# Retention attention regrouped into units of one batch and four heads, issued in a written-out software pipeline with the routing in pieces between

## The chip, the cores and the metric

The kernel runs on one core of a Trainium2 chip. The metric is the device time of one execution in microseconds (us), lower is better. The core has a matrix engine (PE, with its weight loads shown apart as PEld), a vector engine (DVE), an activation engine (ACT), a general engine (POOL) and a queue engine (SP). Each takes its instructions in the order in which they were issued to it. Matmuls write to PSUM, which has eight banks of 128 partitions by 2 KB; DVE and ACT read it, POOL does not in this kernel.

## The reference

The first half is a causal retention over 8 batches, 8 heads, 576 positions and a head dimension of 64. The second half sends each of the 4608 resulting rows of 512 to two of eight small networks.

```python
scores = scale * np.matmul(q, k.transpose(0, 1, 3, 2))
Dmat = np.where(rel >= 0, gamma[:, None, None] ** rel[None, :, :], 0.0)
attn = np.matmul(scores * Dmat, v)              # 8, 8, 576, 64
x = attn.transpose(0, 2, 1, 3).reshape(4608, 512)
logits = x @ w_gate
noisy = logits + np.log1p(np.exp(x @ w_noise)) * noise
top2 = np.argpartition(-noisy, 2, axis=1)[:, :2]
...
    h = np.maximum(x[mask] @ w1[e], 0.0)        # 512 -> 1024
    out[mask] += top2_w[mask, k, None] * (h @ w2[e])
```

## The kernel before

There are two stages. The first reads q, k and v, computes the retention and the routing, and writes the rows, with their routing data, to a scratch array `xd`. The second (`experts`, L581) goes through 40 tiles of 256 rows, five per network: it gathers the rows of a tile from `xd`, multiplies by both weight matrices, and scatters the result.

**Attention.** The work is cut into 16 units, a pair of batches (`bp`) by a pair of heads (`hp`). The decay is split into a factor on v (table `vg`) and a factor on the output (table `gt`), so scores need only a causal mask. The first 512 positions of a head are four chunks of 128; the last 64, the tail, go with both batches in one block. Position 256c + 2p + r lies in partition p (0 to 127) of the loaded tile, so one loaded partition holds two neighbouring positions, and a chunk of 128 positions lies in 64 partitions. `stage_a` (L164) therefore moves data between partition halves while it casts to bf16: eight POOL instructions per unit make `kn` (L180), two on POOL and two on DVE make `vn` (L184), two on ACT make `qb` (L188). It then transposes q and k on PE and copies them out with ACT (L203, L210). `stage_b` (L218) makes the scores S (L230) and masks them on DVE (L233), and makes the running key-value state T per batch (L247), which ACT copies out block by block (L253). `stage_c` (L257) adds, per chunk, vn times S (L272, two 64-column matmuls) and state times q (L275) in PSUM, and DVE writes it out times `gt` as `xT` (L277). The tail has its own small instructions in every unit (L192 to L194, L212 to L215, L239, L240, L282 to L287).

**Routing.** After every fourth unit `route` (L313) takes one `xT` of 1152 rows: 36 small matmuls (L322), a long chain of small DVE instructions, nine POOL additions that depend on each other (`cum`, L368), wide one-hot compares (L432 to L440), 18 matmuls that sum into one PSUM tile `pT` (L443), and for each of nine blocks four transposes, an ACT copy, a POOL copy and a DMA to `xd` (L449 to L453). After the last one `finish` (L455) and `overflow_list` (L466) make the lists.

**Order.** In the attention and the routing a scheduler orders the instructions of each engine by its own priorities, so the order in the source isn't the order on the chip: the trace shows instructions of `route` among those of later units, and the weight loads of the first three networks (`load_weights`, L788, called at units 7, 9 and 11) are issued from 23.45 us on. All q, k and v loads and the writes to `xd` go through SP's queue. In `experts` the order is written out by hand (`manual_schedule`, L740), except for eleven DVE memsets ahead of it (L598, L600). There the weights of networks 3 to 7 come through a staging buffer (`wload`, L605) and ACT casts (`wcast`, L621); the first five tiles load none.

PSUM tiles by name and number of buffers: `tr` 2 (transposes), `S` 2, `x` 2, `T` 1 (states, and the small results of the routing), `pT` 1.

Of the kernel before, what the change touches and what calls it, by code (L numbers as in the profile page):

```python
# [39 lines left out]
def constants(nc, cp):  # L40
# [47 lines left out]
def decay_tables(nc, cp, tmp):  # L88

    vg = cp.tile([P, 4, 2, 2, 2, 2], F32, name="vg")  # L90
# [8 lines left out]
    nc.gpsimd.iota(sv, pattern=[[1, 2], [256, 2]], base=0, channel_multiplier=2,  # L99
# [16 lines left out]
class Attention:  # L116
    def __init__(self, tc, ctx, K, q, k, v):
# [5 lines left out]
        self.raw = ep("at_raw", 2)  # L123
# [5 lines left out]
        self.vg, self.vgt, self.gt = decay_tables(nc, self.cp, self.bf)  # L129
        self.Tb = [self.cp.tile([P, 4, P], BF16, name=f"Tb{j}") for j in range(4)]  # L130
        for t in self.Tb:
            nc.gpsimd.memset(t, 0.0)
        self.u = {}
        self.tails = {}
        self.mains = {}
        self.xT = {}

    def load(self, u):
        nc = self.nc
        bp, hp = u // 4, u % 4  # L140
        d = {}
        for n in "qkv":
            a = self.src[n]
            if hp % 2 == 0:
                r = self.raw.tile([P, 2, 2, 4, P], F32, name=f"raw_{n}")
                for b in range(2):
                    for c in range(2):
                        nc.sync.dma_start(  # L148
                            out=r[:, b, c],
                            in_=a[2 * bp + b, 2 * hp:2 * hp + 4, 256 * c:256 * c + 256, :].rearrange(  # L150
                                "h (p r) d -> p h (r d)", r=2))
                self.mains[n] = r
            d[n] = self.mains[n][:, :, :, (hp % 2) * 2:(hp % 2) * 2 + 2, :].rearrange("p b c h x -> p (b c) h x")
            if hp == 0:
                t = self.raw.tile([P, 8, HD], F32, name=f"rawt_{n}", bufs=1)
                for b in range(2):
                    nc.sync.dma_start(
                        out=t[b * HD:(b + 1) * HD],
                        in_=a[2 * bp + b, :, 512:, :].rearrange("h s d -> s h d"))
                self.tails[n] = t  # L160
            d[n + "t"] = self.tails[n][:, 2 * hp:2 * hp + 2, :]
        self.u[u] = d

    def stage_a(self, u):  # L164

        nc, K = self.nc, self.K
        V = nc.vector
        d = self.u[u]
        hp = u % 4

        kn = self.bf.tile([P, 2, 4, 2, HD], BF16, name="kn")
        vn = self.bf.tile([P, 2, 4, 2, HD], BF16, name="vn")
        rk = d["k"].rearrange("p c h (r d) -> p c h r d", r=2)
        rv = d["v"].rearrange("p c h (r d) -> p c h r d", r=2)
        for cpar in range(2):
            si = slice(cpar * HD, (cpar + 1) * HD)
            for r in range(2):
                so = slice(r * HD, (r + 1) * HD)
                for h in range(2):
                    nc.gpsimd.affine_select(kn[so, cpar, :, h, :], rk[si, :, h, r, :], pattern=[[0, 4], [0, HD]],  # L180
                                            base=1, channel_multiplier=0, compare_op=Alu.is_gt, fill=0.0)
                g = self.vg[si, hp, r].rearrange("p b c h -> p (b c) h").unsqueeze(3).to_broadcast([HD, 4, 2, HD])
                eng = nc.gpsimd if r else V
                eng.tensor_tensor(vn[so, cpar], rv[si, :, :, r, :], g, Alu.mult)  # L184
        qb = self.bf.tile([P, 4, 2, 2, HD], BF16, name="qb")
        rq = d["q"].rearrange("p c h (r d) -> p c h r d", r=2)
        for r in range(2):
            nc.scalar.activation(qb[:, :, r], rq[:, :, :, r, :], Act.Copy, scale=0.125)  # L188
        qt = self.bf.tile([P, P], BF16, name="qt")
        kt = self.bf.tile([P, P], BF16, name="kt")  # L190
        vt = self.bf.tile([P, 2, HD], BF16, name="vt")
        V.tensor_scalar_mul(qt, d["qt"].rearrange("p h d -> p (h d)"), 0.125)  # L192
        V.tensor_copy(kt, d["kt"].rearrange("p h d -> p (h d)"))
        V.tensor_tensor(vt, d["vt"], self.vgt[:, 2 * hp:2 * hp + 2].unsqueeze(2).to_broadcast([P, 2, HD]), Alu.mult)  # L194

        pq = self.ps.tile([P, 2, 2, 2, 2, HD], BF16, name="tr", bufs=2)
        for b in range(2):
            for cc in range(2):
                for r in range(2):
                    nc.tensor.transpose(pq[:, b, cc, :, r, :],  # L200
                                        qb[:, 2 * b + cc, r].rearrange("p h d -> p (h d)"), K["ident"])
        QT = self.tp.tile([P, 8, P], BF16, name="QT")
        nc.scalar.activation(QT, pq.rearrange("p b c e r q -> p (b c e) (r q)"), Act.Copy)  # L203
        pk = self.ps.tile([P, 8, P], BF16, name="tr", bufs=2)
        knv = kn.rearrange("p e (b c) h d -> p e b c (h d)", b=2)
        for b in range(2):
            for c in range(4):
                nc.tensor.transpose(pk[:, 4 * b + c, :], knv[:, c % 2, b, c // 2, :], K["ident"])
        KT = self.tp.tile([P, 8, P], BF16, name="KT")
        nc.scalar.activation(KT, pk, Act.Copy)  # L210
        pt = self.ps.tile([P, 2, P], BF16, name="tr", bufs=2)
        nc.tensor.transpose(pt[:, 0, :], qt, K["ident"])  # L212
        nc.tensor.transpose(pt[:, 1, :], kt, K["ident"])
        TT = self.tp.tile([P, 2, P], BF16, name="TT")
        V.tensor_copy(TT, pt)  # L215
        d.update(kn=knv, vn=vn.rearrange("p e (b c) h d -> p e b c h d", b=2), vt=vt, QT=QT, KT=KT, TT=TT)

    def stage_b(self, u):  # L218

        nc, K = self.nc, self.K  # L220
        V = nc.vector
        d = self.u[u]
        ST = {}
        mk = K["mask"].rearrange("p r q -> p (r q)").unsqueeze(1).to_broadcast([P, 4, P])
# [356 lines left out]
def experts(tc, K, wp, w1, w2, keep, xd, yd, out, W):  # L581
# [7 lines left out]
    with tc.tile_pool(name="moe_g", bufs=1) as gp, \  # L589
# [293 lines left out]
```

## Time and profile before

| | us |
|---|---|
| median of 3 runs (lowest, highest) | 652.82 (652.56, 658.53) |
| profiled execution | 652.35 |
| its span, first to last instruction | 650.8 |
| first masked score (DVE L233) | 26.86 |
| last output of the attention (DVE L287) | 287.23 |
| first gather (POOL L632) | 321.62 |
| first expert matmul (PE L677) | 328.95 |

| engine | busy us | share of the span |
|---|---|---|
| PE | 496.8 | 76% |
| PEld | 325.6 | 50% |
| POOL | 355.9 | 55% |
| DVE | 311.5 | 48% |
| ACT | 285.6 | 44% |

A share over the span mixes two stages with different limits; read each from its own stretch. The time ahead of the first and behind the last instruction is the difference of the profiled execution to its span, 1.55 us. Matmul ends are modelled, so the distance between starts says how fast PE goes, and the granted clock is given as a share of 2.4 GHz: 0.50 is 1.2 GHz.

### The profile page before, as it was taken

The page shows a single profiled execution, that of the slowest core. Times are in us where ns is not written, and L with a number is a line of the kernel's source. Part 1 is how long each engine was busy: PE and PEld are TensorE (multiplying, and loading weights), DVE is VectorE, ACT ScalarE, POOL GpSimd, SP SyncE. Part 2 cuts the span into 40 slices and gives each one's busy share as a digit, 9 for nine tenths or more (in the row PEclk, how much of TensorE's full clock was granted, in tenths as well). Part 3 has the DMA queues.
Part 4 walks back from the last instruction along what each step waited for, and adds up shares of the span by engine and source line. Part 5 has one row for each costly group of instructions (what it writes and reads, how often), then busy time and mean ns, then how long its engine had stood idle before and what let it go on. Part 6 is the DMA issues. An engine that isn't in the chain of part 4 may idle for free.

```text
span 650.8 us, 10530 instructions
## 1 busy us (share of the span) xinstructions
PE 496.8 (76%) x3729; PEld 325.6 (50%) x3729; DVE 311.5 (48%) x820; ACT 285.6 (44%) x457; POOL 355.9 (55%) x493
## 2 busy tenths in 40 slices
PE   0583954877468755870389999999899998999990
PEld 0342432634254424540267666676576665666760
DVE  0544478366835684658422234444344443444440
ACT  4622342732154323430234476576466755644430
POOL 5916526361534335201473067777777777777772
PEclk9999999965577555855679999999899998999996
DMA  9999980777037002000233476877868798666551
GB/s 176 263 225 228 223 237 25 213 207 199 0 108 191 20 1 76 1 1 0 93 88 115 143 237 200 263 238 253 270 206 282 259 300 279 217 193 210 181 188 68
DMA packets 112153, 108.60 MB, mean 167 GB/s; under 512 B 28707, under 2 KB 85540, under 8 KB 112097
## 3 DMA queue, kind: packets, MB, share of 16 engines
q1 hardware_dynamic: 86384, 72.51, 37.8%
q0 software_dynamic: 20800, 34.97, 20.1%
q10 hardware_dynamic: 4912, 0.41, 0.6%
q8 instruction: 30, 0.49, 0.3%
q14 instruction: 27, 0.21, 0.1%
HBM read 91.21 MB, written 41.83 MB: 204 GB/s over the span
## 4 chain that ended last, share of the span: by engine, by line
PE 54%; DMA 14%; DVE 10%; issue 7%; POOL 6%; ACT 4%; SPq 3%; ACTq 0%; POOLq 0%; DVEq 0%
PE p L677 20%; PE po L696 19%; DMA raw_v<-in_v_dram 4%; SPq L148 3%; DMA prv<-yd,ix 2%; PE pt L661 2%; PE x L272 2%; POOL kn L180 2%; POOL vn L184 2%; PE S L230 2%; DVE vn L184 2%; PE T L247 2%; DVE S L233 2%; DMA xd<-xr 2%; PE pT L443 1%
## 5 line engine op out<-in xcount | busy, mean ns | idle before, releaser
L677 PE MATMUL p<-xgT,w 128*128 128x256 bf16 x1280 | 246.1, 277 | 0.0
L696 PE MATMUL po<-w,hT 128*128 128x512 bf16 x640 | 242.0, 382 | 5.3 <-DVE o L727 5.3
L677 PEld LDWEIGHTS <-w 128*128 128x128 bf16 x1280 | 127.3, 99 | 89.0 <-issue 7.9
L684 DVE TENSOR_SCALAR hT<-p 128x512 bf16<-128x512 f32 x80 | 55.2, 691 | 151.6 <-PE p L677 151.6
L682 ACT ACTIVATE hT<-p 128x512 bf16<-128x512 f32 x80 | 47.8, 597 | 125.3 <-PE p L677 80.1
L705 POOL DMA_INDIRECT prv<-yd,ix x70 | 71.5, 1021 | 49.3 <-DVE hT L684 27.8
L632 POOL DMA_INDIRECT xg<-xd,xi x80 | 80.7, 1008 | 28.9 <-issue 16.8
L180 POOL TENSOR_SCALAR_AFFINE_SELECT kn<-raw_k 64x256 bf16<-64x256 f32 x128 | 62.3, 507 | 52.0 <-PE T L247 28.4
L733 POOL DMA_INDIRECT out_dram<-o,ix x70 | 71.1, 1016 | 21.8 <-issue 15.9
L696 PEld LDWEIGHTS <-hT 128*128 128x128 bf16 x640 | 62.9, 98 | 8.7
L184 POOL TENSOR_TENSOR vn<-raw_v,vg 64x512 bf16<-64x512 f32 x32 | 38.9, 1214 | 42.0 <-DMA raw_v<-in_v_dram 20.0
L727 DVE SCALAR_TENSOR_TENSOR o<-po,f,prv 128x512 f32<-128x512 f32 x70 | 50.1, 744 | 18.7 <-DMA prv<-yd,ix 14.5
L716 ACT ACTIVATE y<-po,f 128x512 f32<-128x512 f32 x80 | 50.5, 683 | 12.0 <-PE po L696 12.0
L247 PE MATMUL T<-vn,kn 128*128 128x512 bf16 (+3 forms) x128 | 39.3, 419 | 20.9 <-POOL vn L184 10.7
L233 DVE TENSOR_TENSOR S<-S,mask 128x512 bf16<-128x512 f32 x64 | 43.0, 685 | 22.1 <-PE S L230 21.6
L451 ACT ACTIVATE xr<-tr 128x512 bf16<-128x512 bf16 x36 | 20.2, 595 | 72.1 <-DMA xd<-xr 32.3
L253 ACT ACTIVATE Tb<-T 64x256 bf16<-64x256 f32 x64 | 24.2, 378 | 57.4 <-PE T L247 57.0
L449 PE MATMUL tr<-ident,xT 128*128 128x128 bf16 x144 | 20.9, 298 | 32.3 <-ACT xr L451 32.2
L664 ACT ACTIVATE xgT<-pt 128x1024 bf16<-128x1024 bf16 x40 | 40.7, 1018 | 10.2 <-DVE f L646 8.7
L368 POOL TENSOR_TENSOR cum<-cum,M 128x8 bf16<-128x8 bf16 x36 | 7.4, 206 | 66.0 <-DVE df L385 31.6
L272 PE MATMUL x<-S,vn 128*64 128x128 bf16 x256 | 42.4, 300 | 0.0
L628 ACT ACTIVATE w<-wst 128x1024 bf16<-128x1024 f32 x40 | 39.9, 1048 | 0.0
(167 smaller groups left out, 598.4 us busy)
## 6 DMA issues: line engine op xcount, KB each, us to landing
wst<-in_moe_w_dram SPq DMA_DIRECT2D x40, 512.0 KB, 6.0
yd<-y SPq DMA_DIRECT2D x35, 512.0 KB, 3.7
raw_q<-in_q_dram SPq DMA_DIRECT2D x32, 256.0 KB, 5.3
raw_k<-in_k_dram SPq DMA_DIRECT2D x32, 256.0 KB, 5.3
raw_v<-in_v_dram SPq DMA_DIRECT2D x32, 256.0 KB, 5.2
w<-in_moe_w_dram POOLq DMA_DIRECT2D x6, 1024.0 KB, 17.0
xd<-xr SPq DMA_DIRECT2D x36, 132.0 KB, 1.8
xg<-xd,xi POOLq DMA_INDIRECT x80, 3.2
```

The source lines that it names most:

```text
L180: nc.gpsimd.affine_select(kn[so, cpar, :, h, :], rk[si, :, h, r, :], pattern=[[0, 4], [0, HD]], base=1, channel_multiplier=0, compare_op=A ...
L184: eng.tensor_tensor(vn[so, cpar], rv[si, :, :, r, :], g, Alu.mult)
L233: V.tensor_tensor(S, p, mk, Alu.mult)
L247: nc.tensor.matmul(p[:, c:, :], lhsT=d["kn"][:, c % 2, b, c // 2, :], rhs=vv.unsqueeze(1).to_broadcast([P, 4 - c, P]), start=(c == 0), sto ...
L272: nc.tensor.matmul(p[s, c, :], lhsT=d["vn"][:, c % 2, b, c // 2, h, :], rhs=ST[b, h][:, c, :], start=(c == 0), stop=(c == 0), skip_group_c ...
L632: nc.gpsimd.indirect_dma_start(out=xgs[i % NX][:, s, :], out_offset=None, in_=xd[:, :], in_offset=IOff(ap=keep["xi"][:, 2 * i + s:2 * i + ...
L677: nc.tensor.matmul(p1[:, f2, :], lhsT=w[:, o:o + P], rhs=xgT[:, di, :], start=(di == 0), stop=(di == KD - 1))
L684: V.tensor_relu(hT[:, 2 * fp:2 * fp + 2, :], p1)
L696: nc.tensor.matmul(po[s], lhsT=hT[:, fi, s * P:(s + 1) * P], rhs=w[:, o:o + DM], start=(fi == 0), stop=(fi == KF - 1))
L705: nc.gpsimd.indirect_dma_start(out=prv[i % NP][:, s, :], out_offset=None, in_=yd[:rows, :], in_offset=IOff(ap=st[i]["ix"][:, s, 1:2], axis=0),
L716: nc.scalar.activation(y[:, s, :], po[s], Act.Copy, scale=g[:, s:s + 1])
L733: ins = nc.gpsimd.indirect_dma_start(out=out[:, :], out_offset=IOff(ap=st[i]["ix"][:, s, 0:1], axis=0), in_=st[i]["o"][:, s, :], in_offset ...
```

## The change

Units are now one batch by four heads (`unit`: bp, half of the heads hq, batch b), still 16. Data stay in the partitions in which they were loaded: position parity r becomes a separate index of the tiles, and partition halves (index e, 64 partitions) are chunks. `kn` is two POOL instructions of 128 partitions, `vn` one POOL instruction, `qb` one on ACT. Scores and the v-times-S product use 64x64 blocks of the PE array, twice as many matmuls as before in each; states use 128- and 64-partition matmuls. The tails of a pair of batches are cast and transposed once for all heads. `route` becomes a generator with a yield after each small piece (32 yields); its PSUM tiles have a bank of their own, `R`, and `pT` is added up in SBUF (`L`) after each route. The whole first stage is issued under `manual_schedule`, in the order of the loop below. Loads run four units ahead. Only networks 0 and 1 are loaded during the attention, in halves; network 2 comes through `wload` in the first five tiles, and `W[2]` lies in a pool of the second stage.

```diff
+    def load(self, u, queues):
...
+            r = self.raw.tile([P, 2, 4, P], F32, name=f"raw_{n}")          # pool at_raw: bufs 2 -> 4
...
+        kn = self.bf.tile([P, 2, 2, 4, HD], BF16, name="kn", bufs=3)
+        rk = d.pop("rawk").rearrange("p c h (r d) -> p (c h) r d", r=2)
+        for r in range(2):
+            nc.gpsimd.affine_select(kn[:, r].rearrange("p c h d -> p (c h) d"), rk[:, :, r, :], ...
+        nc.gpsimd.tensor_tensor(vn.rearrange("p r c h d -> p (c h) r d"), rv,
+                                self.vg[:, hq]....to_broadcast([P, 8, 2, HD]), Alu.mult)
+        nc.scalar.activation(qb.rearrange("p r c h d -> p (c h) r d"), ..., Act.Copy, scale=0.125)
...
+    def tr(self, u, n):
...
+                    nc.tensor.transpose(p[:, hp, c, r, :], src[:, r, c, 2 * hp:2 * hp + 2, :]..., self.K["ident"])
+        nc.scalar.activation(t..., p..., Act.Copy)
+    def scores(self, u, hp):
+        p = [self.ps.tile([P, 2, 2, P], F32, name="S", bufs=2) for h in range(2)]
+        for c in range(2):
             for r in range(2):
                 for h in range(2):
+                    s = slice(h * HD, (h + 1) * HD)
+                    for e in range(2):
+                        nc.tensor.matmul(p[h][e * HD:(e + 1) * HD, c, r, :]...,
+                                         lhsT=d["K"][s, hp, c, r, e, :], rhs=d["Q"][s, hp, c, :, e, :], ...
+        for h in range(2):
+            nc.vector.tensor_tensor(S, p[h], self.K["mask"].unsqueeze(1).to_broadcast([P, 2, 2, P]), Alu.mult)
+    def states(self, u, hp):
+        p = self.ps.tile([P, 4, P], F32, name="T", bufs=1)
+        for c in range(2):
+            for k, n in ((P, slice(2 * c + 1, 4)), (HD, slice(2 * c, 2 * c + 1))):
                 for r in range(2):
+                    nc.tensor.matmul(p[:, n, :], lhsT=d["kn"][:k, r, c, hs, :]..., rhs=m, ...
+        for h in range(2):
+            nc.scalar.activation(T[s, :, s], p[s, :, s], Act.Copy)
+    def out(self, u, e):
+        p = self.ps.tile([P, 2, 2, P], F32, name="x", bufs=2)
+        q = slice(e * HD, (e + 1) * HD)
+        for hp in range(2):
+            for c in range(2):
+                for r in range(2):
+                    for h in range(2):
+                        nc.tensor.matmul(p[s, hp, c, :], lhsT=d["vn"][q, r, c, 2 * hp + h, :],
+                                         rhs=d["S", hp, h][q, c, r, :], ...
+                j = 2 * c + e
+                if j:
+                    nc.tensor.matmul(p[:, hp, c, :]..., lhsT=d["T", hp][:, j - 1, :], rhs=d["Q"][:, hp, c, :, e, :], ...
+        nc.vector.tensor_tensor(xv, p, gv, Alu.mult)
...
+        pT = ps.tile([P, 2 * NH], F32, name="R", bufs=1)
+        if bp:
+            V.tensor_add(self.L, self.L, pT)
...
-            if i < NTE or e >= E or j == NTE - 1:
+            if e >= E or j == NTE - 1:
...
+    with ExitStack() as actx, tc.manual_schedule(engines=order):
+        at.load(0, (nc.scalar, nc.sync, nc.sync))
+        at.load_tail(0, (nc.scalar, nc.sync, nc.sync))
+        for u in (1, 2, 3):
+            at.load(u, (nc.sync,) * 3)
+        K = at.K = constants(nc, cp)
+        at.tables()
...
+        rt = Router(tc, actx, K, at, wgn, moe_noise, xd, keep)
...
+        def step(n=1):
+            for _ in range(n):
+                while pend and next(pend[0], pend) is pend:
+                    pend.pop(0)
+        at.cast(0)
+        at.tr(0, "q")
+        at.tr(0, "k")
+        at.cast(1)
+        at.cast_tail(0)
+        at.tr_tail(0)
+        for n in range(NU + 1):
+            u, p = n, n - 1
...
+            if u + 4 < NU:
+                at.load(u + 4, (nc.sync,) * 3)
+            if n % 4 == 0 and n // 4 < 3:
+                at.load_tail(n // 4 + 1, (nc.sync,) * 3)
+            at.scores(u, 0)
+            step()
+            at.out(p, 0)
+            step()
+            at.tr(u + 1, "q")
+            step()
+            at.scores(u, 1)
+            step()
+            at.out(p, 1)
+            at.cast(u + 2)
+            step()
+            at.tr(u + 1, "k")
+            step()
+            for hp in tails:
+                at.scores_tail(bp, hp)
+            at.states(u, 0)
+            step()
+            for hp in tails:
+                at.out_tail(bp, hp)
+            at.states(u, 1)
+            if prev and p % 4 == 3:
+                pend.append(rt.route(bp))
+            step()
...
+            if n in (5, 7, 9, 11):
+                load_weights(nc, wp, moe_w1, moe_w2, (n - 5) // 4, W, (n - 5) // 2 % 2)
+        while pend:
+            step()
+        rt.finish()
+        rt.overflow_list()
```

(The conditions on the first and the last unit are left out of the loop.)

## Rows read from the trace of the kernel before

**Rows 1.** Page, 40 slices of 16.27 us: busy tenths, granted clock, DMA rate.
```profile
PE   0583954877468755870389999999899998999990
PEclk9999999965577555855679999999899998999996
GB/s 176 263 225 228 223 237 25 213 207 199 0 108 191 20 1 76 1 1 0 93 88 115 143 237 200 263 238 253 270 206 282 259 300 279 217 193 210 181 188 68
```

**Rows 2.** Busy time by stretch: PE, PEld, DVE, ACT, POOL (count), clock, DMA share, GB/s.
```profile
26.90:287.50 260.60, 180.42 (x1383) 106.95 (x1383) 154.37 (x399) 91.56 (x162) 106.61 (x202) 0.77 0.52 127
287.50:328.90 41.40, 9.37 (x83) 7.36 (x81) 24.90 (x97) 9.26 (x15) 13.13 (x24) 0.54 0.14 44
328.90:650.80 321.90, 300.95 (x2227) 207.12 (x2224) 125.92 (x305) 169.82 (x239) 217.67 (x216) 0.96 0.66 211
```

**Rows 3.** Groups by shape, 26.9 to 287.5: count, busy us, mean ns, idle before.
```profile
L180 POOL TENSOR_SCALAR_AFFINE_SELECT kn<-raw_k 64x256 bf16<-64x256 f32 x112 | 55.6, 517 | 45.0 <-PE T L247 28.4 <-PE tr L208 8.2 <-DMA raw_k<-in_k_dram 4.9
L233 DVE TENSOR_TENSOR S<-S,mask 128x512 bf16<-128x512 f32 x64 | 43.0, 685 | 22.1 <-PE S L230 21.6
L184 POOL TENSOR_TENSOR vn<-raw_v,vg 64x512 bf16<-64x512 f32 x31 | 37.5, 1209 | 42.0 <-DMA raw_v<-in_v_dram 20.0 <-issue 11.6 <-PE x L272 9.1
L184 DVE TENSOR_TENSOR vn<-raw_v,vg 64x512 bf16<-64x512 f32 x28 | 24.5, 876 | 8.2 <-DMA raw_v<-in_v_dram 7.8
L253 ACT ACTIVATE Tb<-T 64x256 bf16<-64x256 f32 x64 | 24.2, 378 | 57.4 <-PE T L247 57.0
L277 DVE TENSOR_TENSOR xT<-x,gt 128x512 bf16<-128x512 f32 x32 | 22.0, 689 | 15.3 <-PE x L275 15.2
L240 DVE TENSOR_TENSOR St<-S,maskt 128x128 bf16<-128x128 f32 x32 | 9.2, 289 | 11.0 <-PE S L239 10.6
L368 POOL TENSOR_TENSOR cum<-cum,M 128x8 bf16<-128x8 bf16 x27 | 5.6, 207 | 33.8 <-DVE df L386 21.0 <-DVE d L381 10.9
```

**Rows 4.** Order of time on PE, 24 to 33 us: start, length, line, count.
```profile
24.41 0.62 PE L230 MATMUL S<-QT,KT 64*128 64x128 bf16 x8
...
30.88 0.61 PE L230 MATMUL S<-QT,KT 64*128 64x128 bf16 x4
31.42 0.42 PE L272 MATMUL x<-S,vn 128*64 128x128 bf16 x3
31.77 0.29 PE L275 MATMUL x<-QT,Tb 128*128 128x128 bf16 x1
31.99 0.32 PE L272 MATMUL x<-S,vn 128*64 128x128 bf16 x2
32.23 0.29 PE L275 MATMUL x<-QT,Tb 128*128 128x128 bf16 x1
```

**Rows 5.** Order of time on PE, later: the routing's dense run, transposes, outputs.
```profile
115.72 2.60 PE L443 MATMUL pT<-oh,olo 128*128 128x160 bf16 x18
121.79 0.61 PE L200 MATMUL tr<-ident,qb 128*128 128x128 bf16 x8 [0.60 <-DVE TT L215]
264.27 0.25 PE L272 MATMUL x<-S,vn 128*64 128x128 bf16 x2
264.45 0.23 PE L275 MATMUL x<-QT,Tb 128*128 128x128 bf16 x1
```

**Rows 6.** Busy time by stretch, columns as in Rows 2: the clock up and down.
```profile
186.00:188.00 2.00, 2.00 (x24) 2.00 (x22) 0.07 (x1) 0.40 (x1) 0.23 (x2) 0.66 0.40 138
202.00:204.00 2.00, 0.28 (x2) 0.15 (x3) 0.93 (x2) 0.47 (x2) 1.78 (x5) 1.00 0.31 72
206.00:222.00 16.00, 13.73 (x89) 7.38 (x88) 9.59 (x20) 3.84 (x6) 6.47 (x11) 0.50 0.47 122
260.00:268.00 8.00, 7.20 (x82) 5.00 (x81) 5.15 (x12) 5.78 (x9) 3.48 (x8) 1.00 0.01 2
```

**Rows 7.** Groups by shape on DVE between the last output and the first expert matmul.
```profile
L600 DVE MEMSET prv<- 128x1024 f32 x4 | 3.6, 912 | 0.6 <-issue 0.6
L598 DVE MEMSET xg<- 128x528 f32 x7 | 3.5, 498 | 0.7 <-DVE xT L287 0.3
```

More of the change, by code (lines that the diff above doesn't have):

```diff
@@ L128, in __init__ @@
         self.ps = ep("at_ps", 1, space=bass.MemoryType.PSUM)
[L129 to L132, printed above, removed]
+        self.Tb = [self.cp.tile([P, 4, P], BF16, name=f"Tb{j}") for j in range(8)]
         self.u = {}
         self.tails = {}
-        self.mains = {}
+        self.T = {}
         self.xT = {}
-    def load(self, u):
-        nc = self.nc
-        bp, hp = u // 4, u % 4
-        d = {}
[L142 to L162, printed above, removed]
@@ L164, in stage_a, with unit @@
-    def stage_a(self, u):
-        nc, K = self.nc, self.K
-        V = nc.vector
-        d = self.u[u]
[L169 to L176, printed above, removed]
+    @staticmethod
+    def unit(u):
+        return u // 4, u // 2 % 2, u % 2
@@ new lines, in tables @@
+    def tables(self):
+        self.vg, self.vgt, self.gt = decay_tables(self.nc, self.cp, self.bf)
+        for t in self.Tb:
+            self.nc.gpsimd.memset(t, 0.0)
+    def load(self, u, queues):
+        bp, hq, b = self.unit(u)
+        d = self.u[u] = {}
+        for n, q in zip("qkv", queues):
+            r = self.raw.tile([P, 2, 4, P], F32, name=f"raw_{n}")
+            for c in range(2):
+                q.dma_start(out=r[:, c], in_=self.src[n][2 * bp + b, 4 * hq:4 * hq + 4, 256 * c:256 * c + 256, :].rearrange(
+                    "h (p r) d -> p h (r d)", r=2))
+            d["raw" + n] = r
@@ L182, in stage_a @@
[L182 to L189, printed above, removed]
@@ L202, in stage_a @@
[L202 to L210, printed above, removed]
@@ new lines, in states @@
+    def states(self, u, hp):
+        nc = self.nc
+        d = self.u[u]
+        bp, hq, b = self.unit(u)
+        p = self.ps.tile([P, 4, P], F32, name="T", bufs=1)
+        hs = slice(2 * hp, 2 * hp + 2)
+        first = True
+        for c in range(2):
+            for k, n in ((P, slice(2 * c + 1, 4)), (HD, slice(2 * c, 2 * c + 1))):
+                for r in range(2):
+                    m = d["vn"][:k, r, c, hs, :].rearrange("p h d -> p (h d)").unsqueeze(1).to_broadcast(
+                        [k, n.stop - n.start, P])
+                    nc.tensor.matmul(p[:, n, :], lhsT=d["kn"][:k, r, c, hs, :].rearrange("p h d -> p (h d)"), rhs=m,
+                                     start=first, stop=(c == 1 and k == HD and r == 1), skip_group_check=True)
+                    first = False
+        T = self.Tb[(2 * u + hp) % 8]
+        for h in range(2):
+            s = slice(h * HD, (h + 1) * HD)
+            nc.scalar.activation(T[s, :, s], p[s, :, s], Act.Copy)
+        d["T", hp] = self.T[bp, b, 2 * hq + hp] = T
```

291 lines of the change are left out of this document (167 added, 124 removed).

## The prediction

> **What bounds the kernel now.** I read the page's slices first: PE is at 0.9 and the clock at full from slice 20 on, and both are ragged before [rows 1]. The busy times by stretch put numbers on this [rows 2]. From 328.9 us on PE works 301 of 321.9 us at clock 0.96: the expert stage is bound by PE, and the change leaves its arithmetic alone. From 26.9 to 287.5 us no engine is full: PE 180 of 260.6 us, DVE 154, POOL 107, ACT 92. That is 16.3 us per unit. Then 41.4 us pass in which PE has 9.4 us of work: the last route, the lists and the first gathers, a chain.
>
> The groups by shape say why no engine is full [rows 3]: POOL waits 28.4 us for a buffer that PE's states still read and 20.0 us for v; ACT waits 57 us for PE's states, DVE 22 us for scores. The engines wait for each other in turn, with two buffers between them. The loads run at about 225 GB/s until slice 7, where 12 MB of weights stand among them, and are nearly idle later [rows 1]; they don't set the end.
>
> The clock is the second thing to see. Its row says full speed until slice 8, yet the 18 matmuls of 160 columns at 115.72 us take 2.60 us [rows 5], 1.2 columns per ns: half speed. After this run the eight transposes at 121.79 us start some 0.06 us apart, full speed. So 1.00 ahead of the first change in the record is no measurement. Later the clock rises at 186 to 188 us, in another such run, holds at PE 90% busy with 82 short matmuls in 8 us, falls after 2 us in which PE had 0.28 us of work, and doesn't rise in the 16 us from 206, though PE shows 13.7 us busy there [rows 6].
>
> **PE's price per unit.** Starts give passes and switches. Four score matmuls take 0.54 us to the next start (30.88 to 31.42), one 128x128 pass 0.22, a pair on the two column halves 0.24, three of them 0.35 [rows 4]. With 0.107 us per pass of 128 columns at half speed, this fits if two matmuls on different halves run together and each change of the array's shape costs 0.11 us. The eight scores at 24.41 last as long as four, so row halves run together too. At full speed the pair takes 0.18 us [rows 5]: 0.055 for the pass, about 0.10 for the switch.
>
> In the new unit I count: q and k transposes 16 passes, 2 switches; scores 32 matmuls, 16 passes if two run at a time, 2 switches; states 24 passes, 8 switches (128 and 64 partitions alternate); outputs 32 in pairs and 6 full, 22 passes, 4 switches; tails, averaged, 6 passes, 3 switches. Together 84 passes and 19 switches: 9.0 + 2.1 = 11.1 us at half speed, 4.6 + 1.9 = 6.5 us at full. No row shows four blocks at once. If four scores run together, 8 passes less, 0.9 us; if none run together, 32 passes more (16 in the scores, 16 in the outputs), 3.4 us. I take pairs, which the rows show.
>
> Routing on PE is 9.4 us per route at clock 0.54 [rows 2], so 2.4 us per unit, and about 1.5 at full speed. The one `T` buffer adds a wait: the second state waits for two ACT copies of 0.38 us [rows 3] and the hand-over, say 0.9 us. In-order waits for DVE or POOL behind a route piece I put at 0.5 us per unit: between 0 and 4, since POOL may hold `cum` (9 x 0.21 us) behind a whole cast. That makes 11.1 + 0.9 = 12.0 us for a unit without routing and 14.9 with it at half speed, 9.4 with it at full.
>
> **The other engines per unit.** DVE: four masks of 0.69, two outputs of 0.69, per unit three tail pieces of 0.29, 5.0 us [rows 3]; routing at most (24.9 - 7.1 of memsets) / 4 = 4.5 us [rows 2, 7]; together 9.5. The DVE half of `vn` (0.88 x 2) and the tail casts go. ACT keeps its copies and gets the tail cast, some 7 us; no queue of it fills. POOL: `kn` 2 instructions at twice the elements, 0.52 to 1.03 each; `vn` 1.2 to 2.4 us; so 2.2 to 4.5 us, I take 4.2, hidden under 12 us of PE. For a two-input operation the Trainium skill (GPSIMD Engine Reference, Engine selection) expects POOL to take about twice DVE's time, which speaks against moving all of `vn` there. The rows have 1209 against 876 ns, 1.4 times, so the trace disagrees. By the rule `vn` would take 3.5 us, `cum` would wait 1.1 us longer in each route, and the end would move by some 4 us.
>
> DMA: a unit is six loads of 256 KB and a quarter of the tails, 1.8 MB, 7.9 us at 225 GB/s [rows 1]; below 12 us. Weights drop from 12 to 8 MB and move to units 5 to 11, out of the way of the first loads. SP carries loads and `xd` writes in one queue, so a block written behind a burst of 1.6 to 2.3 MB lands up to 10 us late, and with three `xr` buffers ACT and then the transposes wait. Only the last blocks of route 0 meet a burst (at n = 8): 0 to 8 us once, inside the 0.5 us per unit.
>
> **The sum.** Start: the first score is at 26.9 us [rows 2]. It stays about there (24 to 30): ACT has its tables and ten noise loads ahead of the first q cast, while the loads get ahead. n = 0: 8 us, filling. n = 1 to 4: 4 x 12.0 = 48. n = 5 to 7, half speed: 3 x 14.9 = 44.7. By then the 18 `pT` matmuls and the row transposes of route 0 have run; rows 6 show that such runs raise the clock and that ordinary attention work holds it until PE stands idle. I take half of the eight units n = 8 to 15 at full speed. There DVE's 9.5 is the larger, and with the waits I take 10.8: 4 x 14.9 + 4 x 10.8 = 102.8. n = 16, outputs alone: 5. The last output is at 26.9 + 8 + 48 + 44.7 + 102.8 + 5 = 235 us, against 287.5.
>
> From there to the first expert matmul the chain is the same, 41.4 us now. The scheduler put the 7.1 us of memsets between its links [rows 7]; in written order they come behind the lists, where the first (0.5 us) holds the first gather. But DVE has 7 us less in the chain. I take 43 (37 to 50). Experts: 8 DMAs and 8 casts for network 2 in four tiles that loaded nothing, as later tiles do at PE 0.9 and above: 0, between 0 and 3 us. Experts start at 278 instead of 328.9: 51 us less. 652.35 - 51 = 601 us; the profiled execution is 0.5 us below the median. I say 600.
>
> **Rivals.**
> *The clock stays up.* The order keeps PE fed and no gap lets it fall. n = 1 to 4 are then held by loads and hand-overs at 10 us, the rest by DVE at 10.3: 26.9 + 8 + 40 + 113.3 + 5 + 41 = 234, 95 us less, 557 us. For it: the 8 us at full clock from 260 [rows 6]. Against: 16 us of busy PE at half clock from 206.
> *The clock stays down.* 26.9 + 8 + 48 + 11 x 14.9 + 5 + 43 = 295, 34 us less, 618 us; with two more in-order waits of 1 us per unit, 640. For it: row runs of 64x64 blocks with switches are what didn't raise it at 206. What transposes do for a rise no row separates; by the Trainium skill (TensorE: Matmul & The Clock Gate, PE-mode transpose) they don't count as busy in the same way, and if so the row transposes don't help, which speaks for this 618.
> *No gain.* The written order puts PE in line behind every late route piece. If each of the eight pieces between two units costs 0.5 us, 4 us per routed unit, 44 us of the 51 go: about 645 (no change is 646 to 659). For it: PE now waits for `cum`, DVE and ACT in each route; against: the pieces are small and the state of one lies a step behind the other.
> *Slower: blocks run one by one.* If the 64 half-array matmuls of scores and outputs don't overlap, 32 passes more, 3.4 us in each of 16 units, 55 us on the half-speed case: 673. It decides from where the 16 scores of one call take over 1.5 us. Against: pairs in both directions in rows 4.
>
> **How the numbers follow.** The forecast's case 0.48 (its own range 588 to 616), clock up 0.20, clock down 0.16, no gain 0.07, one by one 0.09. The range reaches over the forecast, most of the clock's two cases and the unknown waits: 554 to 632. A change within 1% (6.5 us) can't be told from none in this kernel. Faster by over 1%: 0.48 + 0.20 + 0.16 = 0.84; within 1%: 0.07; slower: 0.09.
>
> **What would show it.** The last `xT` output near 235 us and the first expert matmul near 278. Scores of 16 matmuls some 1.0 us long at half clock. PE nearly full between, DVE near 9.5 us per unit. Clock 0.5 until the first `pT` run, then changing. It is wrong if units take over 15 us, if PE waits long for POOL or `xr`, or if the gap to the experts grows beyond 50 us.

## The result and the profile after

| us | before | forecast | after |
|---|---|---|---|
| median of 4 runs (lowest, highest) | 654.45 (652.56, 658.53) | 600 | 628.00 (626.40, 632.19) |
| first masked score | 26.9 | 26.9 | 35.8 |
| last output of the attention, its end | 287.5 | 235 | 263.9 |
| first expert matmul | 328.9 | 278 | 310.3 |
| from there to the end | 321.9 | 321.9 | 320.4 |

The ratio to the kernel before is 0.960 [0.953, 0.967]: faster, but by 26 us where I forecast 52. Some executions of a kernel take over 1.5% longer than its fastest, and the ratios leave these out. The profiled execution of the changed kernel took 632.19 us. The whole difference to the forecast, 32 us in that execution, arises ahead of the first expert matmul. The page's slices (40, of 15.8 us; compare [rows 1]):

```profile
PE   0179985757657966604499999999896999999990
PEclk9999975565658555856599999999998999999996
GB/s 196 239 267 290 189 151 118 6 219 146 266 27 102 45 2 1 135 76 63 89 160 161 216 273 211 249 231 259 251 273 278 161 287 331 194 198 213 175 190 88
```

Counted from 0, PE is full in slices 3 and 4 and then ragged; the clock is mostly near 0.5 from slice 6 to slice 19. Busy times by stretch, columns as in [rows 2]: units n = 0 to 4; n = 5 to 7; n = 8 to the last output; the gap; the experts.

```profile
35.80:83.90 48.10, 43.90 (x522) 28.17 (x521) 21.12 (x41) 24.46 (x38) 14.97 (x16) 1.00 1.01 236
83.90:128.40 44.50, 31.54 (x378) 21.92 (x376) 29.77 (x82) 18.02 (x29) 15.18 (x24) 0.58 0.41 85
128.40:263.90 135.50, 94.34 (x1123) 62.63 (x1124) 71.81 (x196) 53.86 (x91) 30.44 (x64) 0.61 0.41 98
263.90:310.30 46.40, 9.95 (x95) 7.79 (x93) 27.74 (x98) 9.80 (x16) 13.49 (x26) 0.55 0.27 93
310.30:630.60 320.30, 296.53 (x2186) 206.17 (x2224) 126.00 (x304) 176.93 (x247) 217.20 (x215) 0.97 0.66 218
```

Without routing PE works 44 of 48 us. The clock's 1.00 there is the record ahead of its first change, no measurement; the length of equal groups shows half speed until 77 us and full speed from there to 84, with the first matmul of a route at 83.0 (eight transposes, sixteen scores, eight transposes):

```profile
75.99 1.06 PE L222 MATMUL tr<-ident,qb 128*128 128x128 bf16 x8
76.98 0.44 PE L238 MATMUL S<-QT,KT 64*64 64x128 bf16 x16
78.04 0.61 PE L222 MATMUL tr<-ident,kn 128*128 128x128 bf16 x8
```

With routing PE works 126 of 180 us. Between the first masks of successive units pass 7.9, 9.7, 11.0, 10.7, 8.8 (n = 0 to 4), 10.7, 18.6, 15.2, 25.5 (n = 5 to 8), 10.7, 18.6, 14.5, 18.0 (n = 9 to 12), 10.7 and 17.0 us: of four units with one route in them, one is short and three are long. Of the long ones n = 6 first, in order of time on PE, then on VectorE (DVE):

```profile
94.68 0.22 PE L413 MATMUL R<-M,ltri 128*128 128x72 bf16 x1 [1.14 <-DVE M L405]
96.90 0.22 PE L415 MATMUL R<-cum,ones 128*128 128x72 bf16 x1 [2.00 <-POOL cum L410]
...
99.22 0.64 PE L238 MATMUL S<-QT,KT 64*64 64x128 bf16 x16
99.66 1.06 PE L283 MATMUL x<-S,vn 64*64 64x128 bf16 x16
...
103.46 0.26 PE L307 MATMUL S<-TT 64*128 64x128 bf16 x1 [1.35 <-DVE S L243]
104.06 0.26 PE L307 MATMUL S<-TT 64*128 64x128 bf16 x1 [0.33 <-DVE S L243]
107.35 0.46 PE L307 MATMUL S<-TT 64*128 64x128 bf16 x2 [3.03 <-DVE St L308]
```
```profile
102.74 1.27 DVE L243 TENSOR_TENSOR S<-S,mask 128x512 bf16<-128x512 f32 x2
103.93 0.28 DVE L440 TENSOR_TENSOR MM<-MM,R 128x144 f32<-128x144 f32 x1
...
106.93 0.18 DVE L464 CAST hib<-hi 128x18 bf16<-128x18 f32 x1
107.02 0.48 DVE L308 TENSOR_TENSOR St<-S,maskt 128x128 bf16<-128x128 f32 x2
```

PE waits for `M` and `cum`, then three times with the tail scores (L307) for a free `S` bank: twice for the masks at 102.74, and 3.03 us for the tail mask at 107.02, which stands on DVE behind fifteen small instructions of the route (103.93 to 106.93) and one output. In n = 7 the `pT` run waits 3.54 us for `oh`. In n = 8 it is the rows. SP's queue, then ACT and PE:

```profile
129.14 1.15 SPq L153 DMA_DIRECT2D raw_q<-in_q_dram  x2
...
139.55 1.59 SPq L161 DMA_DIRECT2D rawt_v<-in_v_dram  x2
141.25 7.36 SPq L514 DMA_DIRECT2D xd<-xr  x6
```
```profile
144.33 0.60 ACT L512 ACTIVATE xr<-tr 128x512 bf16<-128x512 bf16 x1 [9.24 <-DMA xd<-xr]
```
```profile
144.98 1.01 PE L222 MATMUL tr<-ident,kn 128*128 128x128 bf16 x8 [7.59 <-ACT xr L512]
```

The writes of `xd` wait behind twelve loads, three `xr` buffers fill, ACT waits 9.24 us, and the k transposes of the next unit wait 7.59 us for the `tr` buffer that this copy reads.

### The profile page after: what moved, and what is told of

Read it like the earlier page. It is cut to its first block, busy times and chain, and to the rows that moved or that the text cites. A ratio compares the mean times of both kernels' runs of the same rounds, so it can differ in the third digit from the quotient of the medians.

```text
span 630.6 us, 11565 instructions
## 1 busy us (share of the span) xinstructions
PE 479.9 (76%) x4329; PEld 329.6 (52%) x4369; DVE 277.4 (44%) x727; ACT 296.5 (47%) x449; POOL 313.3 (50%) x393
## 4 chain that ended last, share of the span: by engine, by line
PE 57%; DVE 14%; DMA 10%; issue 6%; ACT 4%; POOL 4%; SPq 3%; ACTq 0%; POOLq 0%; DVEq 0%
PE p L738 20%; PE po L757 18%; PE T L260 5%; DMA xd<-xr 3%; PE x L283 3%; DMA prv<-yd,ix 2%; PE pt L722 2%; PE tr L222 2%; SPq L153 2%; PE R L498 2%; DVE olo L482 2%; DVE S L243 1%; DMA out_dram<-o,ix 1%; PE S L238 1%; DMA rawt_q<-in_q_dram 1%
## 5 line engine op out<-in xcount | busy, mean ns | idle before, releaser
L757 PE MATMUL po<-w,hT 128*128 128x512 bf16 x600 | 226.5, 381 | 6.3 <-DVE o L788 6.3
L794 POOL DMA_INDIRECT out_dram<-o,ix x70 | 71.1, 1016 | 21.4 <-issue 13.1
L243 DVE TENSOR_TENSOR S<-S,mask 128x512 bf16<-128x512 f32 x64 | 41.1, 683 | 82.2 <-PE S L238 82.2
L260 PE MATMUL T<-vn,kn 64*128 64x128 bf16 (+2 forms) x256 | 51.7, 324 | 8.2 <-ACT Tb L266 8.2
L178 POOL TENSOR_TENSOR vn<-raw_v,vg 128x1024 bf16<-128x1024 f32 x16 | 30.4, 1902 | 43.0 <-PE x L283 25.3
L173 POOL TENSOR_SCALAR_AFFINE_SELECT kn<-raw_k 128x512 bf16<-128x512 f32 x32 | 22.1, 716 | 58.5 <-PE T L260 37.5
L513 POOL COPY xr<-pl 128x8 f32<-128x8 f32 x36 | 9.9, 292 | 77.9 <-DMA xd<-xr 62.1
L689 ACT ACTIVATE w<-wst 128x1024 bf16<-128x1024 f32 x48 | 47.8, 1047 | 0.0
L260 PEld LDWEIGHTS <-kn 128*128 128x128 bf16 (+1 forms) x256 | 18.3, 108 | 39.9 <-issue 36.1
L222 PE MATMUL tr<-ident,qb 128*128 128x128 bf16 x128 | 15.9, 300 | 29.6 <-ACT qb L182 29.6
```

The lines of the kernel that those rows point to most:

```text
L243: nc.vector.tensor_tensor(S, p[h], self.K["mask"].unsqueeze(1).to_broadcast([P, 2, 2, P]), Alu.mult)
L260: nc.tensor.matmul(p[:, n, :], lhsT=d["kn"][:k, r, c, hs, :].rearrange("p h d -> p (h d)"), rhs=m, start=first, stop=(c == 1 and k == HD a ...
L689: nc.scalar.activation(W[e][:, k * F:(k + 1) * F], t, Act.Copy)
L757: nc.tensor.matmul(po[s], lhsT=hT[:, fi, s * P:(s + 1) * P], rhs=w[:, o:o + DM], start=(fi == 0), stop=(fi == KF - 1))
L794: ins = nc.gpsimd.indirect_dma_start(out=out[:, :], out_offset=IOff(ap=st[i]["ix"][:, s, 0:1], axis=0), in_=st[i]["o"][:, s, :], in_offset ...
```

## The experiments

All runs but after and e14 to e17 were made on two chips (e0 and e7 to e9 on one, the others on the second) on which the expert stage takes some 80 us longer for this kernel (402.0 us in e0_after), so the first stage is compared by its places in the trace; its last output agrees across the chips within 4 us (263.9 and 260.1). Ratios are to the kernel before on the same chip at the same time; a row without one is a single execution. In us:

| run | first mask | last mask | last output | first expert matmul | ratio |
|---|---|---|---|---|---|
| after | 35.8 | 249.5 | 263.9 | 310.3 | 0.960 [0.953, 0.967] |
| e0_after | 35.3 | 245.8 | 260.1 | 306.6 | 0.960 [0.951, 0.970] |
| e1_noise | 23.8 | 233.6 | 248.0 | 294.5 | 0.940 [0.929, 0.951] |
| e2_xr6 | 35.2 | 230.2 | 243.2 | 288.9 | 0.935 [0.925, 0.945] |
| e3_warm | 35.4 | 242.5 | 259.8 | 305.2 | 0.960 [0.951, 0.970] |
| e6_memset | 35.5 | 242.5 | 256.2 | 299.0 | 0.956 [0.949, 0.963] |
| e7_sched | 28.9 | 210.3 | 220.4 | 260.3 | 0.912 [0.903, 0.921] |
| e8_noroute | 35.2 | 155.5 | 164.8 | | |
| e9_nowait | 35.8 | 241.4 | 250.8 | | |
| e10_best | 21.4 | 216.2 | 230.0 | 267.3 | 0.895 [0.880, 0.910] |
| e11_light | 35.5 | 202.8 | 215.5 | | |
| e12_freedve | 35.0 | 234.3 | 249.2 | 294.3 | |
| e13_freepe | 33.3 | 223.5 | 230.9 | 271.4 | |
| e14_pefix | 21.0 | 214.3 | 223.1 | 257.6 | 0.879 [0.875, 0.883] |
| e15_sched6 | 28.7 | 207.5 | 219.9 | 253.2 | 0.884 [0.879, 0.889] |
| e16_fixes | 23.8 | 217.4 | 230.6 | 271.8 | 0.907 [0.903, 0.911] |
| e17_nowait6 | 35.4 | 220.2 | 229.7 | | |

**The start.**

> The changed kernel with the ten noise loads issued from SP, behind the first loads, instead of from ACT. Theory (the start was late because ACT issues the noise loads ahead of the first q cast, from 16.5 to 28.4 us): the first masked score comes near 25 us instead of 35.8, the end 7 to 9 us earlier, about 620. Rival (the q, k, v loads set the start and the early units): the first score moves by less than 3 us, or the units after it wait for loads and give the gain back; the end moves by less than 3 us.

```diff
-                nc.scalar.dma_start(out=self.noise[...], in_=nq[:, j, :, c, :])
+                nc.sync.dma_start(out=self.noise[...], in_=nq[:, j, :, c, :])
```

The first mask came 11.5 us and the last output 12.1 us earlier than in e0_after, more than the 7 to 9 us of the theory. In the changed kernel ACT's queue shows why:

```profile
16.48 5.38 ACTq L341 DMA_DIRECT2D noise<-in_moe_noise_dram  x4
...
28.45 1.06 ACT L182 ACTIVATE qb<-raw_q 128x1024 bf16<-128x1024 f32 x1 [15.30 <-DMA noise<-in_moe_noise_dram]
```

**The rows.**

> The changed kernel with six instead of three buffers for the rows that go to the scratch array. Theory (PE waits for the copies of the rows, these for buffers that wait for writes queued behind loads: 25.3 us for n = 8 and 17.8 us for n = 12, where n = 9 and 13 take 10.5): n = 8 falls to some 16 us and n = 12 to some 13, the last route's rows gain 1 to 2, the end is 10 to 14 us earlier. Rival (the clock and PE's own work set these stretches): below 4 us.

```diff
-        self.rows = ctx.enter_context(tc.tile_pool(name="rtx", bufs=3))
+        self.rows = ctx.enter_context(tc.tile_pool(name="rtx", bufs=6))
```

n = 8 fell from 25.2 (e0_after) to 11.1 us, n = 12 from 17.5 to 12.7, n = 9 rose from 10.7 to 15.7: the last output came 16.9 us earlier, more than the theory asked. 1.2 us of it arise in n = 0 to 4, before any rows.

**The clock at the start.**

> The changed kernel with 96 matmuls of 512 columns put on PE ahead of the first transposes, while PE has nothing to do (about 4 to 29 us); nothing reads their result. Theory of the prediction (once up, the clock is held by attention work until PE stands idle): units n = 0 to 4 run at full clock, 8 us instead of 9 to 11, and the first units end 6 to 10 us earlier, unless loads hold them. Rival (the clock falls by itself under the new mix of short matmuls): n = 1 to 3 take 9.7 to 11 us as now at clock 0.5, end unchanged within 2 us.

```diff
+        for _ in range(96):
+            nc.tensor.matmul(pw, lhsT=K["ident"], rhs=..., start=True, stop=True)   # 512 columns
```

The units n = 0 to 4 took 42.3 us against 45.2 in e0_after, but against 44.0 in e1_noise and e2_xr6, which have no such matmuls; the last output moved by 0.3. The run doesn't answer its question, since the clock was down before the units began. Busy times, columns as in [rows 2]:

```profile
26.00:34.00 8.00, 1.71 (x20) 1.45 (x21) 0.00 (x0) 4.46 (x5) 1.90 (x1) 0.76 1.10 268
34.00:46.00 12.00, 10.83 (x137) 7.16 (x136) 4.70 (x8) 6.29 (x9) 1.27 (x2) 0.50 1.12 244
50.00:54.00 4.00, 4.00 (x93) 3.11 (x92) 2.89 (x5) 2.40 (x4) 1.82 (x3) 1.00 0.99 277
58.00:62.00 4.00, 4.00 (x61) 2.87 (x64) 1.94 (x3) 1.53 (x4) 1.27 (x2) 0.50 1.03 276
```

PE had 1.71 us of work in the 8 us ahead of the first scores, and the units began at half clock. Later the clock rose by itself and had fallen again by 58 us, though between 50 and 58 us PE waited 0.8 us in all: the theory's "until PE stands idle" doesn't describe this fall.

**The gap.**

> The changed kernel with the eleven memsets ahead of the experts on POOL instead of DVE. Theory (they stand one by one between the links of the last route's chain on DVE, from 266 to 275 us): the gap from the last output to the first expert matmul falls from 46.6 to about 41 us (two of them come among POOL's additions, 2 us back), the end 4 to 6 us earlier. Rival (the chain waits there for ACT's tables anyway): below 2 us.

```diff
-            nc.vector.memset(prv[j], 0.0)        # xgs likewise
+            nc.gpsimd.memset(prv[j], 0.0)
```

From the last output to the experts pass 42.8 us instead of 46.5. In the changed kernel the memsets still stand between the links of the chain:

```profile
272.45 0.17 DVE L394 SCALAR_TENSOR_TENSOR nl<-M,nl 128x72 f32<-128x72 f32 x1
272.78 0.91 DVE L661 MEMSET prv<- 128x1024 f32 x1 [0.16 <-issue]
273.61 0.17 DVE L381 TENSOR_REDUCE bm<-nl 128x9 f32<-128x72 f32 x1
```

**The baseline, and the price of routing.**

> The changed kernel once more, as the baseline on the chip on which the next three run. In its own trace the first masked score starts at 35.8 us, the last mask at 249.5, the last output at 263.6 and the first expert matmul at 310.3. Within 3 us of these here: the stages can be compared across chips. Further off: only the traces of this call are compared with each other.

It came out within 4 us, not within 3. The gap lies in n = 2 and 3 (9.9 and 8.6 us here, 11.0 and 10.7 there); from n = 5 on the units agree within 0.5 us. e1, e2, e3 and e6 were not made together with e0_after, so in them a difference of a few us in the first five units shows nothing.

> The routes of the first three pairs of batches are left out (27 blocks of xd are filled with zeros behind the loop, and 27 of 36 blocks of rows reach no network); only the first stage is read. It gives the price of the attention alone. If the written order and the hand-overs set the pace (theory A for the clock: only the waits behind route pieces let it fall), the units run at about 10 us until the clock rises and at 7 to 8 us after, last mask at 175 to 190 us. If attention alone never raises the clock (theory B: the rises come from the pT runs and the row transposes), all 16 units take 9.7 to 11 us at a granted clock of 0.5, last mask at 190 to 205 us. Either way the routing's price in the changed kernel is 249.5 less this time, divided by three: my forecast had 2.9 us per routed unit at half clock (2.4 of TensorE's work and 0.5 of waits), 11.6 per route; the trace makes me expect 15 to 20.

```diff
-                pend.append(rt.route(bp))
+                if bp == 3:
+                    pend.append(rt.route(bp))
```

The attention alone takes 7.9 us per unit (117.8 us between the first masks of n = 0 and n = 15); the last mask at 155.5 is 20 us earlier than even theory A has it. The clock rises without any route and holds for 55 us, so theory B for the clock is refuted. Theory A's condition, that only waits behind route pieces let it fall, fails too: it falls at 119.6 us without any, and from 109 to 120 us no wait of PE was over 0.9 us. Busy times from 65.0 us, where the record rises, to the fall:

```profile
65.00:119.60 54.60, 47.82 (x812) 31.18 (x808) 33.26 (x69) 36.31 (x57) 29.59 (x29) 1.00 1.03 225
```

The three routes cost (245.8 - 155.5) / 3 = 30 us each in the written order, against the 11.6 of my forecast and the 15 to 20 that I expected here.

**The waits for the route's producers.**

> The matmuls of pr (2 per route) and pT (18 per route) read constant tiles (identity and zeros) in place of M, cum, olo and oh. VectorE and GpSimd do all their work as before, but TensorE no longer waits for it at these places; the routing data are then no routing, so only the stretch up to the last output (263.6 us before this edit) is read. Theory A, TensorE's in-order waits behind the route pieces are the loss, and each wait lets the clock fall: the units n = 6, 7, 10, 11, 14, 15 lose their waits of 1.1 + 2.0 us (pr) and 3.5 us (pT), 6.6 us per route, 20 us over three routes, and 5 to 15 us more where the clock then holds; last output at 230 to 245 us. Theory B, VectorE's load in these units is the loss (14 us of its work in the unit with the long chain) and TensorE only shows it: the waits move to the masks and tail scores, last output at 255 us or later, granted clock as before.

```diff
-                nc.tensor.matmul(pT, lhsT=olo[:, j, c, :], rhs=oh[:, j, c]...,
+                nc.tensor.matmul(pT, lhsT=K["ident"], rhs=self.zb[:, :2 * NH],     # pr likewise
```

The last output came at 250.8, between the two theories: 9.3 us earlier, and n = 6 and n = 10 (19.0 us each) were not shorter at all.

> e9_nowait (pr and pT read constant tiles; the routing data are no routing, only the first stage is read) with six xr buffers, as e11_light has them; against e11_light it differs by VectorE's pieces behind pr alone. If the gains add: last output at 260.1 - 9.3 (e9) - 16.9 (e2) = 234 us, and VectorE's chain is worth 234 - 215.5 = 18 us, 6 per route. If the xr wait had only hidden the waits on the producers, it falls further, to 222 to 228, and the chain is worth under 12.

With six buffers it came at 229.7, 13.5 us ahead of e2_xr6: between the two expectations.

**VectorE's chain.**

> Written order, six xr buffers, pr and pT reading constant tiles as in e9_nowait, and VectorE's pieces behind pr left out (from the gate values to the wide compares, about 12 us of VectorE work per route, with its exponential on ScalarE; the routing data are zeros, so only the stretch up to the last output is read). The number of pieces and all of TensorE's work stay. In e9_nowait the unit n = 6 still took 19.0 us and n = 10 too, without the waits for the route's producers. Theory B, it is VectorE's bunched work: n = 6, 7, 10, 11 fall to 9 to 12 us each, last output at 205 to 222 us. Theory A', TensorE's route matmuls and row transposes with the falling clock make the units long by themselves: n = 6 above 15 us, last output above 230.

```diff
-        d = col("d")
-        V.tensor_sub(d, m2, m1)
...
-        V.tensor_scalar_mul(oh[:, :, :, 0, :], oh[:, :, :, 0, :], K["pidx"][:, 0:1])
+        for _ in range(10):
+            yield
```

n = 6 and n = 10 fell to 11.1 and 11.2 us, the last output to 215.5: theory B. The busy times of n = 6 in the changed kernel, in e17_nowait6 and in e11_light (DVE is the third engine):

```profile
94.55:113.19 18.64, 11.79 (x130) 7.45 (x131) 13.96 (x50) 5.66 (x10) 8.26 (x16) 0.50 0.49 101
```
```profile
92.66:111.69 19.03, 11.14 (x128) 7.13 (x126) 16.99 (x49) 6.06 (x10) 8.21 (x16) 0.59 0.47 100
```
```profile
92.80:103.92 11.12, 10.74 (x122) 6.75 (x122) 5.65 (x14) 4.41 (x8) 7.92 (x18) 0.50 0.84 172
```

With PE's waits for `M` and `cum` gone DVE is busy 17.0 of 19.0 us; without the chain 5.7 of 11.1, and PE is full. The chain behind `pr` costs 229.7 - 215.5 = 14.2 us, 4.7 per route.

From the first mask of n = 8 to the last output alone, e0_after, e2_xr6, e17_nowait6 and e11_light, each with one more edit than the one before (columns as in [rows 2]):

```profile
125.20:260.10 134.90, 93.49 (x1121) 62.89 (x1121) 71.80 (x196) 53.70 (x91) 30.29 (x64) 0.61 0.41 99
124.00:243.20 119.20, 85.19 (x1121) 57.72 (x1121) 71.74 (x196) 54.11 (x91) 28.73 (x60) 0.69 0.48 111
120.90:229.70 108.80, 78.87 (x1121) 54.07 (x1121) 75.20 (x196) 54.07 (x91) 30.45 (x61) 0.75 0.56 124
114.80:215.50 100.70, 82.58 (x1122) 55.99 (x1123) 48.76 (x120) 54.27 (x90) 28.12 (x64) 0.71 0.58 134
```

**The written order.**

> The regrouped attention and the route pieces as in the changed kernel, but the first stage's order is left to the scheduler, as it was before the change (the line of manual_schedule is taken away; the expert stage keeps its own). Theory A, the written order puts TensorE in line behind late route pieces and costs more than it saves: faster than the changed kernel by 10 to 25 us. Theory B, the order is part of the gain, since units of TensorE work of 11 us need each other as cover: slower than the changed kernel, by 5 to 25 us, up to the time of the kernel before. Rival: no difference within 5 us, the gain is the regrouping's alone.

```diff
-    with ExitStack() as actx, tc.manual_schedule(engines=order):
+    with ExitStack() as actx:
```

Theory A, and more than it asked: 668.54 us against 706.83 (e0_after) and 735.49 (before) on that chip. Of the change, everything but the written order (the regrouping, the route's pieces and banks, the loads) gives 67 us, and the written order takes 38 back. The scheduler's order has losses of its own: in e7_sched n = 1 takes 21.0 us, with PE waiting 12.0 us for `KT`.

> The written order for every engine but VectorE, whose order in the first stage is left to the scheduler. With all engines free (e7) the last output stood at 220.4 us instead of 260.1, and the first mask at 28.9 instead of 35.3. Theory B, VectorE's order (fourteen microseconds of route pieces and masks bunched into every fourth unit, tail masks behind them) is the loss: last output at 225 to 240 us. Theory A, TensorE's order (matmuls of the route and tail scores standing in line ahead of the next unit's work) is the loss: within 6 us of 260.

> The written order for every engine but TensorE, whose order in the first stage is left to the scheduler. Theory A: TensorE does later transposes, states and scores where it now waits for the route's producers; last output at 225 to 240 us, and a granted clock that holds longer between 84 and 245 us. Theory B: TensorE's results still wait for VectorE in its written order; within 6 us of 260. Both far below 260: each order alone costs, and freeing one is enough.

```diff
+    with ExitStack() as actx, tc.manual_schedule(engines=order - {nc.tensor.engine}):   # e12: nc.vector.engine
```

Freeing DVE alone gave 10.9 us, between the theories; freeing PE alone 29.2, as theory A has it. PE's place in line is the larger part. This doesn't contradict e11_light: DVE is late, and PE's order says who waits for that.

**Do the causes add up, and what beats both?** The edits are those above, combined.

> The written order with three edits together: noise loads issued by SyncE, six xr buffers, the memsets of the expert stage's tiles on GpSimd. Alone they moved the first expert matmul from 306.6 us by 12.1, 17.7 and 7.6 us. If the causes are separate: last output at 231 us, first expert matmul at 270 to 277, about where my forecast had them (235 and 278), ratio to the kernel before 0.90 to 0.92. If the earlier start only lengthens the waits behind loads (units n = 3, 4 and 8), half of the noise edit's 12 us is lost: first expert matmul at 280 or later.

The first expert matmul came at 271.8, 34.8 us earlier than in e0_after where the three edits alone add up to 37.4: separate causes. The median is 593.25 us.

> A version meant to beat both kernels: the regrouped attention with the scheduler's order (e7), noise loads issued by SyncE (e1: first mask 12 us earlier under the written order) and six xr buffers (e2: 16 us under the written order). The scheduler's version has its first mask at 28.9 us and waits for xd writes only 17 us in sum between 84 and 215 us, against 53 in the written order, so both edits are worth less here: 4 to 6 us for the noise loads and 3 to 8 us for the buffers. Last output at 206 to 214 us, ratio to the kernel before 0.89 to 0.90 on this chip (e7: 0.912). Rival: the loads of the first units set the pace there (its DMA share is 1.0 up to 84 us), then under 3 us and 0.91.

The last output missed by 16 us. The scheduler put the noise loads, now SP's, ahead of the q load of a coming unit: in SP's queue they take from 25.96 to 44.04 us, the q load follows at 44.95, and PE waits 15.85 us for it, until 60.27. The early start was lost.

> All engines in the scheduler's order (e7), six xr buffers and memsets on GpSimd, noise loads left on ScalarE. In e10_best the noise loads on SyncE had the first mask at 21.4 us, but TensorE then waited 15.9 us for a q load at 44 us, so that the last output came at 230 instead of e7's 220.4. If the noise loads did that: last output at 212 to 220 and first expert matmul at 250 to 258 here, ratio 0.88 to 0.90. If it was the six xr buffers (another order of the scheduler's): about 230 as in e10_best.

As if the noise loads did it: 219.9 and 253.2, though this kernel also differs from e10_best in the memsets.

> The three edits of e16_fixes, and TensorE's order left to the scheduler (e13_freepe, which alone moved the last output from 260.1 to 230.9). If TensorE's in-order waits are a cause of their own: last output at 208 to 218 us and first expert matmul at 248 to 258, ratio about 0.88. If they were mostly the xr and noise waits seen from TensorE: last output at 222 to 231, little below e16_fixes.

The last output at 223.1 is the second case: most of PE's 29 us was the same time as the waits for `xr`. The gap is shorter, though, 34.5 us against e16's 41.2. 576.82 us (574.67 to 579.25) is the fastest of all, 12% below the kernel before, with e15_sched6 at 579.39 (573.42 to 589.51) not apart from it. Its stretch from 66.9 us to the last output, and two pieces of it:

```profile
66.90:223.10 156.20, 140.96 (x1543) 91.62 (x1541) 112.69 (x283) 73.15 (x121) 49.06 (x89) 0.60 0.60 137
175.00:181.40 6.40, 6.33 (x126) 4.57 (x116) 4.33 (x11) 3.58 (x7) 3.56 (x6) 1.00 0.20 67
181.60:186.00 4.40, 4.40 (x59) 3.31 (x56) 3.69 (x8) 2.38 (x4) 1.90 (x1) 0.50 0.00 0
```

PE is 90% busy, at a granted clock of 0.60: by these figures mostly the clock is left there, with 15 us of waits. At 181.5 us the clock falls although PE was busy all but 0.07 us since 175. Why it holds at 88% busy in e8_noroute and not here isn't settled.

## Why the forecast was right in direction and wrong in size

- **Start, 26.9: wrong by 8.9 us.** I named the ten noise loads ahead of the first q cast and gave them 24 to 30 us all the same. They take 11.5 us (e1_noise).
- **n = 0 to 4, 56 us: measured 48.1.** PE's price per unit was a little high: n = 2 and 3 take 11.0 and 10.7 us, not 12.0. Sixteen scores at half clock take 0.44 us to the next start (99.22 to 99.66), 4 passes of 0.107: four blocks run together, the 0.9 us that I had left out. The wait on the one `T` buffer is 0.92 us, as said. And n = 4, 8.8 us, ran mostly at full clock, before any `pT` run: the sign "clock 0.5 until the first `pT` run" failed.
- **n = 5 to 7, 44.7: measured 44.5, by luck.** n = 5 took 10.7 and n = 6 and 7 took 18.6 and 15.2.
- **n = 8 to 16, 107.8: measured 135.5, the step that failed.** Two terms in it. The in-order waits, 0.5 us per unit (0 to 4), and in them the load burst "0 to 8 us once": with six buffers this stretch is 15.7 us shorter, since the burst meets the rows of routes 0 and 1 (134.9 in e0_after, 119.2 in e2_xr6), and without the waits for the route's producers another 10.4 (e17_nowait6). And DVE's 9.5 us per unit is right as a mean (8.1, 14.0, 7.8 and 5.5 us in n = 5 to 8, mean 8.8) but lands in one unit of four, where it holds the masks and PE behind it: without the chain the stretch is 8.1 us shorter again, 100.7 (e11_light), below the forecast. This is the mechanism of the rival *No gain*, PE in line behind late pieces, at part of its price. Two of the signs of being wrong came: units of 18.6 and 25.5 us, and PE's wait behind `xr`.
- **Half of n = 8 to 15 at full clock: by time 0.71 (59.6 us at 0.50, 43.2 at 1.00), 0.61 granted.** It is 0.69 with six buffers and 0.75 with the waits out as well (e17_nowait6), where the stretch takes 108.8 us, about the 107.8 of the forecast. That attention work can hold the clock was right (e8_noroute, 55 us). That it holds it until PE stands idle was not: it falls at 119.6 us in e8_noroute and at 181.5 in e14_pefix without a long wait of PE. What lets it fall stays open. With waits, chain and buffers out (e11_light) each route still costs (215.5 - 164.8) / 3 = 16.9 us, 7.5 more than its 9.4 of PE work [rows 2]. That the lower clock in the attention is the rest is argued, not shown. The Trainium skill's rule on transposes (TensorE: Matmul & The Clock Gate, PE-mode transpose) stays open: no run took the q and k transposes out; e8_noroute shows only that the row transposes aren't needed for a rise.
- **Gap, 43: measured 46.4.** I had the memsets come behind the lists in written order. They stand ahead of the expert stage's hand-written part, and DVE did them inside the chain; 3.7 us of it (e6_memset).
- **POOL, 4.2 us per unit: measured 3.3**, 2 x 0.716 for `kn` and 1.902 for `vn`. For twice the elements of [rows 3], 1.902 is 1.1 times DVE's 876 ns doubled; but DVE's times in the kernel before go from 674 to 1521 ns, so its mean can hold waits, and against the shortest, doubled, it is 1.4 times. The factor of two that the Trainium skill gave (GPSIMD Engine Reference, Engine selection) isn't reached either way. POOL was no bound.

Added up: 8.9 - 7.9 - 0.2 + 27.7 + 3.4 = 31.9 of the 32.3 us by which the experts start later than forecast.

## What to carry to other kernels

Spread a side chain by its load on each engine in each unit, not by its mean: a mean of 9 us in units of 12 was 14 us in one unit and 5.5 two units later. When an order is written by hand, ask of each instruction that can wait what stands behind it, queues included: here a load burst ahead of small writes and ten small loads ahead of the first cast cost 29 us together, more than the 26 that the change gained. Try the scheduler's order of the same code before keeping one's own; here it was 38 us better.

## What was not expected of the hardware

A small VectorE instruction with two inputs in SBUF waited for GpSimd's whole `vn`: 1.86 us instead of 0.18, twice in the changed kernel.

```profile
100.68 0.16 DVE L436 TENSOR_TENSOR r<-r,df 128x9 f32<-128x9 f32 x1
100.88 1.86 DVE L437 TENSOR_TENSOR pl<-r,pl 128x9 f32<-128x9 f32 x1
102.66 0.16 DVE L438 TENSOR_SCALAR pl<-w 128x9 f32<-128x9 f32 x1
```
```profile
100.81 1.90 POOL L178 TENSOR_TENSOR vn<-raw_v,vg 128x1024 bf16<-128x1024 f32 x1 [1.65 <-PE x L283]
```

The Trainium skill (SBUF — State Buffer, Who interferes with whom) has VectorE and GpSimd share one pair of ports under an exclusive lock, with which these rows agree.
